# The last layer's input product as 15 block products in place of 18

## The chip, the cores and the metric

One core of one Trainium2 chip. The metric is the device time of one execution of the program in microseconds; lower is better. The kernel before took 1162.59 us (median of 3 runs, 1161.39 to 1164.65).

## The reference

Three layers in a row, on 4 x 768 tokens of width 384:

```python
attn_out = _attn_ref(q, k, v, beta)          # delta rule, 8 heads of 48
x = attn_out.transpose(0, 2, 1, 3).reshape(B * S, H * D)
# gated layer: d_ff 1536
xn = x / rms * rms_g
x = (silu(xn @ w_gate) * (xn @ w_val)) @ w_out
# last layer: d_ff 2048
h = x @ w_in
sp = np.where(h > 20.0, h, np.log1p(np.exp(np.minimum(h, 20.0))))
return (h * np.tanh(sp)) @ w_out2            # h * tanh(softplus(h)) is Mish
```

## The kernel before

A block is 64 positions of each of the 4 batches, T = 256 tokens; there are NR = 12. A matrix of 384 columns lies as KD = 3 tiles of 128 partitions. Every float32 operand of a large product is held as a high part (rounded to float32r) and a low part (the rest, by a subtraction on GpSimd), and a product of two operands takes three matmuls: high x high, high x low, low x high (`up`, lines 295 to 301).

`phase_b1` computes the attention row by row, with the first two of six pairs of gated column tiles (256 columns each) beside it, whose sums go to DRAM as `p_d`. `phase_b2` (line 1290) computes the other four pairs for each block: per pair 18 matmuls for the gate, Silu on ScalarE, 18 for the value, a multiplication (L357) and a cast (L360) on VectorE, the low part on GpSimd (L361), and then, after the first pair of the next block, the down product of the block before (72 matmuls). `finish` adds `p_d` (L1315), splits the sum (L1316, L1317) and stores both parts to DRAM (`yh_d`, `yl_d`). Beside it run the conversions of the last layer's weights, which come as 64-bit floats: `prepare_half` unpacks half a tile with one ScalarE instruction (L208) and four on VectorE (L212, L215, L220, L223), casts on ScalarE (L234) and subtracts on GpSimd (L237). All of w_in2 stays in SBUF; most of w_out2 goes through DRAM (`wq_d`) and is loaded during the last block.

`phase_c` is the last layer. A unit is a block and a pair of column tiles: 18 matmuls of 256 columns into one PSUM tile `ph` (a bank), Mish on ScalarE (L1362), a cast on VectorE (L1367), a subtraction on GpSimd (L1368), and 4 units later 12 matmuls of 384 columns (L1380 to L1382) that add to the block's two output banks. Three units are begun ahead of the last gated down product (`between`).

The order of the instructions on each engine is the order of the program text (`manual_schedule`); each engine executes its own in order, and so does each queue of DMA issues (SP's and ScalarE's). `merge` interleaves streams by the units that they yield: the gated products against the conversions, whose budget is CVB1.

## Time and profile before

| | |
|---|---|
| time of the profiled execution | 1162.49 us |
| its span, first to last instruction | 1160.8 us |
| median of the runs | 1162.59 us |
| attention, with gated pairs beside it | to about 441 us |
| gated layer, four pairs | about 441 to 741 us |
| last layer | about 741 us to the end |
| TensorE busy, matmuls | 1104.4 us, 14712 |
| VectorE, ScalarE, GpSimd busy | 616.4, 385.8, 414.5 us |

One execution, taken by the hardware profiler. Matmuls are pipelined: the duration shown is longer than the distance to the next. PE is TensorE's matmuls, PEld its weight loads, DVE VectorE, ACT ScalarE, POOL GpSimd, SP the engine that issues most DMAs. PEclk is the granted clock of TensorE as a share of full speed.

### The profile page before, as it was taken

Reading aid. Unit: us, or ns where it says so; the run is one execution under the profiler, and the core shown is the slowest. Engines: PE = TensorE matmul, PEld = TensorE weight load, DVE = VectorE, ACT = ScalarE, POOL = GpSimd, SP = SyncE. Lnnn points to the kernel's source line nnn. Section 1 sums busy time; section 2 is a strip of 40 time slices with the busy share of each in tenths; the row PEclk is TensorE's granted clock in tenths of the full one; section 3 lists DMA queues with packets and bytes.
Section 4 is the critical chain, followed back from the end, with each engine's and each line's share of the span. In section 5 each row is a group of like instructions: output and inputs, shape, how many; then the busy total and the mean of one; then the engine's idle time right before and its main releaser. Section 6 shows DMA issues by size and latency. Waiting matters only on the chain.

```text
span 1160.8 us, 33146 instructions
## 1 busy us (share of the span) xinstructions
PE 1104.4 (95%) x14712; PEld 1073.8 (93%) x14712; DVE 616.4 (53%) x1032; ACT 385.8 (33%) x829; POOL 414.5 (36%) x370
## 2 busy tenths in 40 slices
PE   5888689999999999999999999999999999999998
PEld 5777679989898899999999999999999999999998
DVE  7855998989898988767777622221111111111110
ACT  4465637576657742122222200111111111111110
POOL 2020234536342653444445422243333322233331
PEclk7666799999999999999999999999999999999999
DMA  9032323334136654344445423501111001111101
GB/s 167 5 79 63 111 56 85 85 84 97 45 91 175 202 180 137 120 145 132 165 150 188 153 82 128 209 19 41 42 42 41 28 22 34 42 41 42 41 3 26
DMA packets 130847, 104.48 MB, mean 90 GB/s; under 512 B 81008, under 2 KB 113264, under 8 KB 130704
## 3 DMA queue, kind: packets, MB, share of 16 engines
q1 hardware_dynamic: 118608, 78.77, 24.6%
q10 hardware_dynamic: 12096, 23.60, 6.0%
q8 instruction: 115, 1.88, 0.7%
q14 instruction: 28, 0.23, 0.1%
HBM read 69.31 MB, written 33.03 MB: 88 GB/s over the span
## 4 chain that ended last, share of the span: by engine, by line
PE 78%; DVE 12%; ACT 4%; issue 2%; POOL 1%; DMA 1%; SPq 1%; POOLq 0%; DVEq 0%; ACTq 0%
PE ph L300 6%; PE ph L299 6%; PE ph L301 6%; PE pd L1381 6%; PE pd L1382 6%; PE pd L1380 6%; PE pv L299 4%; PE pd L333 4%; PE pg L299 4%; PE pg L300 4%; PE pv L300 4%; PE pv L301 4%; PE pd L334 4%; PE pg L301 4%; PE pd L335 4%; DVE pr L700 2%
## 5 line engine op out<-in xcount | busy, mean ns | idle before, releaser
L1368 POOL TENSOR_TENSOR gl<-t,gh 128x512 fp32r<-128x512 f32 x96 | 123.7, 1290 | 266.1 <-DVE gh L1367 266.1
L1367 DVE CAST gh<-t 128x512 fp32r<-128x512 f32 x96 | 43.5, 456 | 328.8 <-ACT t L1362 328.8
L361 POOL TENSOR_TENSOR hl<-sg,hh 128x512 fp32r<-128x512 f32 x72 | 106.2, 1474 | 219.7 <-DVE hh L360 199.0
L1362 ACT ACTIVATE t<-ph 128x512 f32<-128x512 f32 x96 | 57.4, 598 | 346.5 <-PE ph L301 342.8
L300 PE MATMUL ph<-xl,wih 128*128 128x256 f32 x576 | 161.8, 281 | 0.0
L299 PE MATMUL ph<-xh,wih 128*128 128x256 f32 x576 | 161.7, 281 | 0.0
L301 PE MATMUL ph<-xh,wil 128*128 128x256 f32 x576 | 161.6, 281 | 0.0
L1381 PE MATMUL pd<-wql,gh 128*128 128x384 f32 x384 | 129.8, 338 | 0.0
L1382 PE MATMUL pd<-wqh,gl 128*128 128x384 f32 x384 | 129.7, 338 | 0.0
L1380 PE MATMUL pd<-wqh,gh 128*128 128x384 f32 x384 | 129.6, 337 | 0.0
L299 PE MATMUL pg<-xh,wgh 128*128 128x256 f32 x432 | 126.9, 294 | 0.4 <-ACT wgh L234 0.3
L299 PE MATMUL pv<-xh,wvh 128*128 128x256 f32 x432 | 126.0, 292 | 0.0
L301 PE MATMUL pg<-xh,wgl 128*128 128x256 f32 x432 | 123.2, 285 | 0.7 <-DVE wgl L237 0.6
L333 PE MATMUL pd<-hh,woh 128*128 128x256 f32 x420 | 120.8, 288 | 3.3 <-ACT par L1177 3.3
L300 PE MATMUL pg<-xl,wgh 128*128 128x256 f32 x432 | 123.2, 285 | 0.5 <-POOL xl L1127 0.5
L351 ACT ACTIVATE sg<-pg 128x512 f32<-128x512 f32 x72 | 43.2, 600 | 238.4 <-PE pg L301 225.2
L300 PE MATMUL pv<-xl,wvh 128*128 128x256 f32 x432 | 122.4, 283 | 0.0
L301 PE MATMUL pv<-xh,wvl 128*128 128x256 f32 x432 | 122.4, 283 | 0.0
L334 PE MATMUL pd<-hl,woh 128*128 128x256 f32 x420 | 118.9, 283 | 0.0
L335 PE MATMUL pd<-hh,wol 128*128 128x256 f32 x420 | 118.7, 282 | 0.0
L301 PEld LDWEIGHTS ph<-xh,wil 128*128 128x128 f32 x576 | 108.6, 189 | 0.0
L300 PEld LDWEIGHTS ph<-xl,wih 128*128 128x128 f32 x576 | 108.5, 188 | 0.0
(212 smaller groups left out, 2611.0 us busy)
## 6 DMA issues: line engine op xcount, KB each, us to landing
raw<-in_moe_w_out_dram SPq DMA_DIRECT2D x28, 384.0 KB, 3.6
raw<-in_moe_w_in_dram SPq DMA_DIRECT2D x16, 384.0 KB, 4.3
kh<-in_k_dram SPq DMA_DIRECT2D x24, 192.0 KB, 3.7
qp<-in_q_dram SPq DMA_DIRECT2D x24, 192.0 KB, 3.7
v<-in_v_dram SPq DMA_DIRECT2D x48, 96.0 KB, 3.3
raw<-in_moe_w_gate_dram SPq DMA_DIRECT2D x12, 384.0 KB, 4.6
raw<-in_moe_w_val_dram SPq DMA_DIRECT2D x12, 384.0 KB, 3.9
xh_d<-xh SPq DMA_DIRECT2D x12, 384.0 KB, 2.7
```

Of the source, the lines that this page charges most:

```text
L299: nc.tensor.matmul(ps[:, f, :], wh[:, kt, sl], xh[:, kt, :], start=(kt == 0), stop=False)
L300: nc.tensor.matmul(ps[:, f, :], wh[:, kt, sl], xl[:, kt, :], start=False, stop=False)
L301: nc.tensor.matmul(ps[:, f, :], wl[:, kt, sl], xh[:, kt, :], start=False, stop=(kt == KD - 1))
L333: nc.tensor.matmul(ps, wh[:, f, sl], hh[:, f, :], start=(i + f == 0), stop=False)
L334: nc.tensor.matmul(ps, wh[:, f, sl], hl[:, f, :], start=False, stop=False)
L335: nc.tensor.matmul(ps, wl[:, f, sl], hh[:, f, :], start=False, stop=last)
L361: nc.gpsimd.tensor_tensor(out=hl, in0=sg, in1=hh.bitcast(F32), op=ALU.subtract)
L1362: nc.scalar.activation(out=t, in_=ps, func=ACTF.Mish)
L1368: nc.gpsimd.tensor_tensor(out=gl, in0=t, in1=gh.bitcast(F32), op=ALU.subtract)
L1380: nc.tensor.matmul(ps, gh[:, f, sl], wh[:, f, :], start=(m + f == 0), stop=False)
L1381: nc.tensor.matmul(ps, gh[:, f, sl], wl[:, f, :], start=False, stop=False)
L1382: nc.tensor.matmul(ps, gl[:, f, sl], wh[:, f, :], start=False, stop=last and f == 1)
```

## The change

The blocks are taken in 6 pairs. For a pair and three column tiles of w_in2 (a triple, of which there are five), the input product is a product of 3x3 by 3x2 blocks: three column tiles by three k, and three k by two blocks. It was 18 block products and is computed by 15, each of a sum of weight blocks and a sum of input blocks, from which the six results come by 20 additions and subtractions. The sixteenth column tile is computed as before.

- The sums of weights are made in the gated layer (`prepare_forms`: 16 additions on VectorE for each triple, 18 blocks in all with the copies, split by ScalarE and GpSimd) and kept in DRAM, but for the first triple's. Those of triples 1 and 2 are loaded during the last gated block; those of 3 and 4 take turns in ten tiles and are loaded anew in every pair (`load_turn`).
- `finish` in the gated layer only adds. After every second block `forms_of` makes 10 sums of its 6 input blocks on VectorE, casts 16 blocks on ScalarE, subtracts on GpSimd and stores to `xf_d`; it runs beside the following gated blocks (`with_forms`), the last pair's beside the last layer. `load_group` brings them back three at a time.
- In the last layer a product is three matmuls into half a PSUM bank. The steps of `O_STEPS` (after which product, result, first operand, sign, second operand) follow on VectorE, with one copy on ScalarE. Mish works in place, the cast is ScalarE's, the output copy too. The output matmuls stand in a queue of tasks (one 128-token tile of one column tile: three matmuls) and are mixed in at 64 for 81 block products.
- All loads of the last layer are issued by SP. The first triple of the first pair stands where the three units stood.

```diff
+X_STEPS = (
+    (9, 0, ('x', 5), 1, ('x', 1)),
+    (12, 1, ('x', 1), 1, ('x', 0)),
...
+X_RAW = (6, 15, 8, 7, 14, 13)
+W_STEPS = (
+    (3, ('a', 1, 0), 1, ('a', 2, 1)),
+    (2, ('a', 1, 2), 1, ('a', 2, 1)),
+    (5, ('a', 0, 1), 1, ('a', 1, 0)),
...
+W_RAW = {1: (1, 2), 4: (2, 1)}
+O_STEPS = (
+    (1, ('u', 0), ('p', 1), 0, None),
+    (1, ('u', 1), ('u', 0), 1, ('p', 0)),
+    (2, ('u', 0), ('u', 0), 1, ('p', 2)),
+    (4, ('u', 0), ('u', 0), 1, ('p', 4)),
+    (4, ('u', 2), ('u', 0), -1, ('p', 3)),
+    (5, ('u', 3), ('u', 2), 1, ('p', 5)),
+    (6, ('u', 4), ('u', 3), 1, ('p', 6)),
+    (6, ('o', 2, 0), ('u', 4), -1, ('p', 4)),
+    (6, ('o', 1, 0), ('u', 1), -1, ('u', 3)),
+    (7, ('o', 1, 1), ('u', 2), -1, ('p', 7)),
+    (8, ('o', 1, 0), ('o', 1, 0), -1, ('p', 8)),
+    (9, ('u', 3), ('p', 9), 1, ('u', 4)),
+    (9, ('o', 2, 1), ('u', 0), 1, ('p', 9)),
+    (10, ('u', 2), ('p', 10), -1, ('u', 3)),
+    (11, ('u', 4), ('u', 2), -1, ('p', 11)),
+    (11, ('o', 0, 0), ('u', 1), 1, ('u', 4)),
+    (12, ('o', 0, 1), ('p', 12), -1, ('u', 2)),
+    (12, ('o', 2, 0), ('o', 2, 0), 1, ('u', 4)),
+    (13, ('o', 2, 1), ('o', 2, 1), -1, ('p', 13)),
+    (14, ('o', 2, 0), ('o', 2, 0), 1, ('p', 14)),
+)
+
+
 def plan(*streams):
 
...
+    xf_d = [dram.tile([128, 2, 16, T], F32, name=f"xf_d{i}") for i in range(NB)]
+    wi_d = {(s, g): dram.tile([128, 2, 3, 128], F32, name=f"wi_d{s}_{g}") for s in range(1, NS) for g in range(5)}
...
+    wq_d = [dram.tile([128, 2, 2, DM], F32, name=f"wq_d{m}") for m in range(NP2)]
...
+        def keep(g, forms):
+            slot = slot_of(g)
+            nc.scalar.copy(slot[:, 0], forms)
+            nc.gpsimd.tensor_tensor(out=slot[:, 1], in0=forms, in1=slot[:, 0].bitcast(F32), op=ALU.subtract)
+            if (s, g) in wi_d:
+                nc.sync.dma_start(out=wi_d[s, g], in_=slot.bitcast(F32))
...
+            elif i == 2:
+                F = [w2i.tile([128, 3, 128], F32, tag="F", name="F", bufs=6) for _ in range(6)]
+
+                def at(x):
+                    return blocks(x[1])[:, x[2]] if x[0] == "a" else F[x[1] // 3][:, x[1] % 3]
+
+                for j, (to, a, sign, b) in enumerate(W_STEPS):
+                    nc.vector.tensor_tensor(out=at(("w", to)), in0=at(a), in1=at(b), op=PLUS[sign])
+                    if j % 2:
+                        yield P["WS"]
+                for to, a in W_RAW.items():
+                    nc.scalar.copy(at(("w", to)), at(("a", *a)))
+                for g in range(5):
+                    keep(g, F[g])
+                    yield P["WK"]
+
+        return [one(i, 3 * s + i) for i in range(3 if s < NS else 1)]
...
-        op = st.enter_context(pool("op2", 1, side="right"))
...
+            if n % 2 == 0:
+                ys[n // 2] = [tpc.tile([128, 2, T], F32, tag="y", name="y", bufs=2 * KD) for _ in range(KD)]
...
+                nc.scalar.dma_start(out=ys[n // 2][o][:, n % 2], in_=p_d[n][:, o, :])
...
             def finish(o, ps):
-                y = pars.pop((n, o))
-                yh = op.tile([128, T], F32R, tag="yh", name="yh", bufs=2)
-                yl = op.tile([128, T], F32R, tag="yl", name="yl", bufs=1)
+                y = ys[n // 2][o][:, n % 2]
                 nc.vector.tensor_tensor(out=y, in0=y, in1=ps, op=ALU.add)
-                nc.vector.tensor_copy(yh, y)
-                nc.gpsimd.tensor_tensor(out=yl, in0=y, in1=yh.bitcast(F32), op=ALU.subtract)
-                nc.sync.dma_start(out=yh_d[n][:, o, :], in_=yh.bitcast(F32))
-                nc.sync.dma_start(out=yl_d[n][:, o, :], in_=yl.bitcast(F32))
+                if n % 2 and o == KD - 1:
+                    forming.append(forms_of(n // 2, ys.pop(n // 2)))
...
+        more = [prepare_forms(s, (lambda g: w0[g]) if s == 0 else staged) for s in range(NS + 1)]
+        more += [prepare_rows(m, staged) for m in range(NP2)]
+        cv = seq(cv, convs(more, early=True), early_loads())
...
+        todo = [lambda g=g: load_w(1, g, in_wb) for g in range(5)]
+        todo += [lambda m=m, x=x: load_q(m, x, in_wb) for m in (0, 1) for x in "hl"]
+        todo += [lambda g=g: load_w(2, g, in_wb) for g in range(5)]
+        todo += [lambda x=x: load_q(2, x, in_wb) for x in "hl"]
+
+        first = [lambda g=g: load_group(0, g) for g in range(4)] + [lambda: load_raw(0)]
...
         def used(n, m):
+            if m == FA:
+                next_x(n + 1)
+            if n >= 4 and (m - FA) % 2 and first:
+                first.pop(0)()
             if n == NR - 1:
-                for _ in range(min(2, len(free))):
-                    load_q(lambda *a, **kw: wbp[0].tile(*a, tag="wb", bufs=WE, **kw))
-
-        part_b = gated((ps_u, [ps_d], hp, tp), range(FA, NP1), range(NR), lambda n: xs[n], finish_b, next_x, between, used)
+                for _ in range(4):
+                    todo.pop(0)()
...
+        def with_forms(part):
+            for i, w in enumerate(part):
+                yield w
+                turn = i % 3 < 2 if len(ys) == 0 else i % 2
+                if forming and turn and next(forming[0], 0) is not None:
+                    forming.pop(0)
+
...
+    def forms_of(j, y):
+
+        us = {}
+
+        def keep(to, t):
+            fx = tpc.tile([128, 2, T], F32R, tag="fx", name="fx", bufs=4)
+            nc.scalar.copy(fx[:, 0], t)
+            nc.gpsimd.tensor_tensor(out=fx[:, 1], in0=t, in1=fx[:, 0].bitcast(F32), op=ALU.subtract)
+            nc.sync.dma_start(out=xf_d[j][:, :, to], in_=fx.bitcast(F32))
...
+        made = [(to, at(("x", i))) for i, to in enumerate(X_RAW)]
+        for _ in range(len(X_RAW) - 2):
+            keep(*made.pop(0))
+            yield
+        for to, u, a, sign, b in X_STEPS:
+            t = tpc.tile([128, T], F32, tag=f"xu{u}", name="xu", bufs=1)
+            nc.vector.tensor_tensor(out=t, in0=at(a), in1=at(b), op=PLUS[sign])
+            us[u] = t
+            made.append((to, t))
+            keep(*made.pop(0))
+            yield
+        while made:
+            keep(*made.pop(0))
+            yield
+
+    def load_group(j, g):
+        i = (5 * j + g) % 6
+        xg[j, g] = []
+        for x, tag in enumerate(("xh", "xl")):
+            if i < 4:
+                t = w2i.tile([128, 3, T], F32R, tag="gx", name="gx", bufs=8)
+            else:
+                t = xp.tile([128, 3, T], F32R, tag=tag, name="gx", bufs=XB)
+            nc.sync.dma_start(out=t.bitcast(F32), in_=xf_d[j][:, x, 3 * g:3 * g + 3])
+            xg[j, g].append(t)
...
     def phase_c():
         st = ExitStack()
-        units = [(n, m) for n in range(NR) for m in range(NP2)]
...
+        by_end = sorted(range(3), key=lambda i: max(n for n, o in enumerate(O_STEPS) if o[1][:2] == ("o", i)))
+        fs = [3 * s + i for s in range(NS - 1) for i in by_end] + [3 * NS] + [3 * NS - 3 + i for i in by_end]
...
+        pairs = [tpc.tile([128, 2, T], F32, tag="fx", name="ou", bufs=4) for _ in range(2)]
+        ou = [pairs[i // 2][:, i % 2] for i in range(4)] + [tpc.tile([128, T], F32, name="ou4")]
+
+        def half_bank():
+            i = halves[0]
+            halves[0] += 1
+            if i % 8 < 4:
+                banks[i % 4] = ps_u.tile([128, 2, T], F32, tag="u", name="ph")
+            return banks[i % 4][:, i % 8 // 4]
+
+        def finish(j, f, t):
+            nc.scalar.activation(out=t, in_=t, func=ACTF.Mish)
+            held.append((j, f, t))
+            if ready[0]:
+                split()
...
+        def split_one(j, f, t):
+            gh, gl = [hp.tile([128, 2, T], F32R, tag=x, name=x) for x in ("gh", "gl")]
+            nc.scalar.copy(gh, t)
             nc.gpsimd.tensor_tensor(out=gl, in0=t, in1=gh.bitcast(F32), op=ALU.subtract)
-
...
+        def down(j, f, tt, gs):
+            if f == fs[0] and tt == 0:
+                acc[:] = [ps_d.tile([128, DM], F32, tag="d", name="pd") for _ in range(4)]
+            gh, gl = (g[:, tt * 128:tt * 128 + 128] for g in gs)
+            wh, wl = (w[:, f % 2, :] for w in W["q", f // 2])
+            ps, last = acc[tt], f == fs[-1]
+            nc.tensor.matmul(ps, gh, wh, start=(f == fs[0]), stop=False)
+            nc.tensor.matmul(ps, gh, wl, start=False, stop=False)
+            nc.tensor.matmul(ps, gl, wh, start=False, stop=last)
+            if last:
+                ob = sums(NS * j + NS).rearrange("p a t -> p (a t)")[:, :DM]
+                nc.scalar.copy(ob, ps)
+                for b in range(2):
+                    t0 = (tt % 2 * 2 + b) * S + (2 * j + tt // 2) * C
+                    nc.sync.dma_start(out=out[t0:t0 + C, :], in_=ob[b * 64:(b + 1) * 64])
+
+        def beside(weight):
+            debt[0] += weight * 64.0 / 81.0
+            while debt[0] >= 1.0:
+                debt[0] -= 1.0
+                if not tasks:
+                    debt[0] = 0.0
+                    break
+                down(*tasks.pop(0))
+
...
+        def triple(j, s):
+            outs, place = {}, {}
+            steps = list(O_STEPS)
+
+            def at(x):
+                if x[0] == "p":
+                    return place[x[1]]
+                if x[0] == "u":
+                    return ou[x[1]]
+                if x[1] not in outs:
+                    outs[x[1]] = sums(NS * j + s)
+                return outs[x[1]][:, x[2]]
+
+            left = [sum(o[1][:2] == ("o", i) for o in O_STEPS) for i in range(3)]
+            for p in range(15):
+                g, k = divmod(p, 3)
+                xh, xl = (t[:, k] for t in xg[j, g])
+                wh, wl = (t[:, k] for t in wt[s][g])
+                ps = place[p] = half_bank()
+                nc.tensor.matmul(ps, wh, xh, start=True, stop=False)
+                nc.tensor.matmul(ps, wh, xl, start=False, stop=False)
+                nc.tensor.matmul(ps, wl, xh, start=False, stop=True)
+                whole = []
+                while steps and steps[0][0] <= p:
+                    _, to, a, sign, b = steps.pop(0)
+                    if b is None:
+                        nc.scalar.copy(at(to), at(a))
+                    else:
+                        nc.vector.tensor_tensor(out=at(to), in0=at(a), in1=at(b), op=PLUS[sign])
+                    if to[0] == "o":
+                        left[to[1]] -= 1
+                        if left[to[1]] == 0:
+                            whole.append(to[1])
+                yield p
+                if p == 1:
+                    while ended:
+                        finish(*ended.pop(0))
+                for i in whole:
+                    (ended if p == 14 else wholes).append((j, 3 * s + i, outs[i]))
+                while wholes:
+                    finish(*wholes.pop(0))
+
+        def single(j):
+            t = sums(NS * j + NS - 1)
+            w, = wt[NS]
+            ps = [half_bank() for _ in range(2)]
+            for i in range(2):
+                for k in range(KD):
+                    g, c = divmod(X_RAW[2 * k + i], 3)
+                    xh, xl = (v[:, c] for v in xg[j, g])
+                    wh, wl = (v[:, k] for v in w)
+                    nc.tensor.matmul(ps[i], wh, xh, start=(k == 0), stop=False)
+                    nc.tensor.matmul(ps[i], wh, xl, start=False, stop=False)
+                    nc.tensor.matmul(ps[i], wl, xh, start=False, stop=(k == KD - 1))
+                nc.scalar.copy(t[:, i], ps[i])
+                yield i
+            finish(j, 3 * NS, t)
+
+        for _ in triple(0, 0):
+            pass
         yield
...
+        wc = [lambda m=m, x=x: load_q(m, x, wbp[-1].tile) for m in (7, 6) for x in "hl"]
+        wc.append(lambda: load_w(NS, 0, wbp[-1].tile))
...
+        ready[0] = True
+        split()
+        for j in range(NB):
+            for s in range(NS):
+                if s == NS - 1:
+                    for _ in single(j):
+                        beside(3)
+                    if j + 1 < NB:
+                        load_raw(j + 1)
+                if s == 1 and j + 1 < NB:
+                    load_group(j + 1, 0)
+                for p in triple(j, s) if j + s else ():
+                    beside(1)
+                    if p % 5 == 0:
+                        next(late, None)
+                    if p % 3 == 2:
+                        if s == 0 and j:
+                            load_turn(NS - 2, p // 3)
+                        if s == NS - 2:
+                            load_turn(NS - 1, p // 3)
+                        if wc:
+                            wc.pop(0)()
+                        if s == NS - 1 and j + 1 < NB and p < 12:
+                            load_group(j + 1, p // 3 + 1)
+        while ended:
+            finish(*ended.pop(0))
+        while tasks:
+            down(*tasks.pop(0))
         st.close()
```

## Rows read from the trace of the kernel before

**Rows 1.** Windows: us, busy time of each engine with instructions, PEclk, DMA share, GB/s.

```profile
461.00:665.00 204.00, 204.00 (x1703) 204.00 (x1702) 144.75 (x232) 44.81 (x90) 94.96 (x86) 1.00 0.46 149
...
741.40:1156.60 415.20, 414.91 (x2955) 414.58 (x2953) 59.08 (x128) 58.55 (x97) 127.25 (x100) 1.00 0.12 37
...
740.00:745.00 5.00, 5.00 (x44) 5.00 (x44) 1.11 (x2) 2.10 (x3) 1.34 (x2) 1.00 0.89 342
```

**Rows 2.** Instruction groups, last layer (700 to 1161 us): busy us, mean ns | idle before.

```profile
L300 PE MATMUL ph<-xl,wih 128*128 128x256 f32 x576 | 161.8, 281 | 0.0
...
L1368 POOL TENSOR_TENSOR gl<-t,gh 128x512 fp32r<-128x512 f32 x96 | 123.7, 1290 | 266.1 <-DVE gh L1367 266.1
...
L1362 ACT ACTIVATE t<-ph 128x512 f32<-128x512 f32 x96 | 57.4, 598 | 346.5 <-PE ph L301 342.8 <-DMA xl<-yl_d 3.6
```

**Rows 3.** Timeline of TensorE in the last layer: start us, us, engine line.

```profile
1041.93 0.28 PE L299 MATMUL ph<-xh,wih 128*128 128x256 f32 x1
...
1044.07 0.33 PE L1380 MATMUL pd<-wqh,gh 128*128 128x384 f32 x1
...
1046.18 0.28 PE L299 MATMUL ph<-xh,wih 128*128 128x256 f32 x1
```

**Rows 4.** Groups, VectorE, gated layer (461 to 665 us).

```profile
L223 DVE SCALAR_TENSOR_TENSOR t<-raw,t 128x384 int32<-128x384 int32 x30 | 33.7, 1125 | 1.0
L215 DVE TENSOR_SCALAR t<-t 128x384 int32<-128x384 int32 x30 | 32.0, 1067 | 1.0
L357 DVE TENSOR_TENSOR sg<-sg,pv 128x512 f32<-128x512 f32 x32 | 21.9, 685 | 31.9 <-PE pv L301 30.4 <-ACT t L208 1.5
L220 DVE SCALAR_TENSOR_TENSOR t<-raw,t 128x384 int32<-128x384 int32 x30 | 20.5, 685 | 0.2
L360 DVE CAST hh<-sg 128x512 fp32r<-128x512 f32 x32 | 13.7, 428 | 1.1
L212 DVE TENSOR_SCALAR t<-t 128x384 f32<-128x384 f32 x30 | 10.6, 352 | 0.0
L1315 DVE TENSOR_TENSOR par<-par,pd 128x256 f32<-128x256 f32 x24 | 10.1, 420 | 23.0 <-PE pd L335 22.9
```

**Rows 5.** Single lines, VectorE and GpSimd: ns min/median/max, first and last start us.

```profile
L652 DVE TENSOR_TENSOR PT<-p,mpos x2: 662/666/671, 48.2 to 48.8; 128x512 f32<-128x512 f32 x2
...
L237 DVE TENSOR_TENSOR wgl<-t,wgh x6: 551/558/560, 115.7 to 370.0; 128x384 fp32r<-128x384 f32 x6
...
L215 DVE TENSOR_SCALAR t<-t x68: 359/780/1360, 102.7 to 656.9; 128x384 int32<-128x384 int32 x68
...
L223 DVE SCALAR_TENSOR_TENSOR t<-raw,t x68: 557/559/1542, 103.7 to 661.4; 128x384 int32<-128x384 int32 x68
...
L1317 POOL TENSOR_TENSOR yl<-par,yh x36: 726/735/989, 464.8 to 757.6; 128x256 fp32r<-128x256 f32 x36
```

**Rows 6.** Groups, whole span, ScalarE.

```profile
L1177 ACT COPY par<-pd 128x256 f32<-128x256 f32 x33 | 12.3, 373 | 37.9 <-PE pd L335 35.1 <-issue 2.5
...
L234 ACT CAST wih<-t 128x384 fp32r<-128x384 f32 x16 | 8.1, 506 | 1.2 <-DVE t L220 0.8 <-DVE t L223 0.4
...
L351 ACT ACT_TABLE_LOAD x1 | 1.3, 1283 | 0.0
L1362 ACT ACT_TABLE_LOAD x1 | 1.3, 1283 | 1.0 <-issue 1.0
```

**Rows 7.** Timeline in the gated layer, VectorE and GpSimd.

```profile
505.70 1.35 DVE L215 TENSOR_SCALAR t<-t 128x384 int32<-128x384 int32 x1
...
505.54 1.29 POOL L361 TENSOR_TENSOR hl<-sg,hh 128x512 fp32r<-128x512 f32 x1 [1.43 <-DVE hh L360]
```

**Rows 8.** Groups, GpSimd, gated layer (461 to 665 us).

```profile
L361 POOL TENSOR_TENSOR hl<-sg,hh 128x512 fp32r<-128x512 f32 x31 | 42.6, 1374 | 68.5 <-DVE hh L360 68.5
L1317 POOL TENSOR_TENSOR yl<-par,yh 128x256 fp32r<-128x256 f32 x24 | 19.4, 807 | 33.7 <-DVE yh L1316 14.7 <-DMA yl_d<-yl 11.6 <-issue 3.6
L237 POOL TENSOR_TENSOR wil<-t,wih 128x384 fp32r<-128x384 f32 x16 | 17.3, 1083 | 4.9 <-ACT wih L234 4.9
```

More of the change, by code (lines that the diff above doesn't have):

```diff
@@ L226, in prepare_half, with part @@
         yield
+    def prepare_half(half, get_pool, key, cut, act, low_by, kw):
+        src, nk, nf = cut
+        rows_split = nk == 2
+        def part(a):
+            return a[:, half:half + 1, :] if rows_split else a[:, :, half * 128:half * 128 + 128]
+        nk1 = 1 if rows_split else nk
+        ts = []
+        yield from value(part(src), nk1, act, ts)
         if half == 0:
```

200 lines of the change are left out of this document (121 added, 79 removed), and 13 rows, old and new, of the table W_STEPS.

## Prediction

> **What bounds the kernel now.** I read the page's slices first, to find where TensorE's line turns solid, then a table of windows over the two solid stages, then instruction groups, then timelines. In the windows [rows 1] see two stretches in which TensorE is busy all the time at a granted clock of 1.00: the gated layer (204.00 us of 204.00) and the last layer (414.91 of 415.20). The other engines differ: VectorE works 144.75 us of the first but only 59.08 of the second, GpSimd 94.96 and 127.25, ScalarE 44.81 and 58.55. No matmul group of the last layer has idle time before it, while ScalarE and GpSimd sit idle ahead of their work until TensorE or VectorE releases it [rows 2]. So in both stages each matmul more or less is its own length more or less, as long as the others keep up.
>
> The length is the distance between starts, not the 281 ns shown as busy, since matmuls overlap. In the timeline [rows 3], 18 matmuls of 256 columns start within 2.14 us (118.9 ns each), the next 12 of 384 within 2.11 (175.8 ns). Other such runs of 12 give 2.08, so I use 174.6. Check: 1728 x 0.1189 + 1152 x 0.1746 + 72 x 0.1189 (the last gated down product, which lies inside) = 205.5 + 201.1 + 8.6 = 415.2 us, the whole window.
>
> **The change part by part.** *Removed matmuls.* Per pair of blocks, the input product was 16 column tiles x 3 k x 2 blocks x 3 = 288 matmuls of 256 columns. Now five triples of 15 products x 3 make 225, the single sixteenth tile 18: together 243. 45 x 6 pairs = 270 fewer, so 270 x 0.1189 = 32.1 us. The 1152 matmuls of the output product stay, with the same operand sizes. All of that lies on the path that sets the end.
>
> *Sums behind the products.* A triple gives VectorE 19 additions (a twentieth step is ScalarE's copy). 16 read one PSUM operand of 128x256, as L1315 does now: 0.420 us [rows 4]. Three read SBUF twice. For these the trace has 0.558 at 384 columns and 0.666 at 512 [rows 5], a slope of 0.84 ns a column, so about 0.45 at 256. One triple: 16 x 0.42 + 3 x 0.45 = 8.1 us. TensorE's share of a triple is 45 x 0.1189 + 11.85 output tasks (15 x 64/81) x 3 x 0.1746 = 5.35 + 6.2 = 11.55 us, or 0.77 per product. VectorE would be 70% busy and keep up on average. ScalarE per pair: 16 Mish at 0.60 [rows 2], 16 casts of 512 columns at some 0.6 (0.506 at 384), 7 PSUM copies at 0.373 [rows 6], 4 output copies near 0.5: 24 us of 62. GpSimd keeps its 16 x 1.29 = 20.6.
>
> What can stall TensorE is PSUM. The eight halves lie in four banks. A product whose turn opens a new tile needs the readers of the products four and eight before it. Four products are about 3.1 us, and VectorE's backlog stays under 0.6, save at one place: product 4 is read again in the second addition of step 6, some 1.05 us after product 6 ends (two additions of 0.42 and hand-overs of about 0.1). Product 8 could start 1.23 us after that end if an output task follows both 6 and 7, but after 0.71 if one is skipped: 0.35 us lost, in some 4 of 10 triples, where product 8 opens a tile (half of them): 2 us in all. The Trainium skill's PSUM page (PSUM — Partial Sum Buffer, "PSUM bank collisions raise a hardware error") says to guard PSUM by bank, not by address, for two engines on one bank. The tiles ph, pg and pv of before are read only whole, so no row shows a half read while the other is written. By that rule product 8 waits in every triple, and the term is 4 us. Bounds without it: 0, and one lost half microsecond in each of 29 triples, 14. I take 3.
>
> *First triple.* It stands alone ahead of the last gated down product, with no output tasks to fill: 5.35 us of matmuls against VectorE's 8.1, behind the last gated multiply and cast (0.685 + 0.43 [rows 4]). Followed by hand, product 8 waits till 4.3 us (instead of 2.9), and the fifteenth ends 1.9 us late. Bounds 0.5 and 8.1 - 5.35 = 2.8. I take 1.9; the down product behind it (8.6 us) lets VectorE catch up.
>
> *Hand-over.* The casts for the first output tasks get their space only when the last down product has read it. Cast 0.6, GpSimd's subtraction 1.29, hand-overs: 2.1 us, of which two products and a first matmul cover 1.0. Cost 1.1, bounds 0 and 2.1. Later tasks have 4 or more others queued in front of each (the order gives 4 to 10 left at every step), about 3.9 us, against a chain of 0.42 + 0.6 + 0.6 + 1.29 and hand-overs, 3.2.
>
> *Gated layer.* TensorE's work is unchanged: 216 matmuls, 25.7 us a block. Beside it, VectorE loses the yh casts and gains 80 additions of weights (128x128, about 0.33 by the same slope) and 50 of the input (0.45); a last 10 fall into the next stage. Conversions now spread over all 12 blocks (their units add up to some 189 of the 192 that the merge allots): 32 x (0.352 + 0.359 + 0.557 + 0.559) = 58.5 us. Per block: 4 x (0.685 + 0.428) + 3 x 0.420 + 58.5/12 + 80 x 0.33/12 + 5 x 0.45 = 15.0 us. But these instructions wait for GpSimd. At 505.70 an L215, 0.359 us when free, takes 1.35 because GpSimd's subtraction began at 505.54 and lasted 1.29 [rows 7]. In the stretch, L223, L215 and L220 average 1.125, 1.067 and 0.685 against 0.559, 0.359 and 0.557 undisturbed [rows 4, 5]: 1.40 us for each of 30, or 5.3 a block (7.94 blocks), 45% of GpSimd's 12.0 us a block. GpSimd will have 4 x 1.29 + 8 x 0.735 + 42 x 1.08/12 = 14.8 us [rows 2, 5, 8]. At 45% VectorE loses 6.6 and needs 21.6 of 25.7: it keeps up, with bursts (16 weight additions at a time). The chain behind the last pair (multiply, cast, subtraction, 2.4 us) has about 6 us until TensorE needs it. I take 2 us; bounds 0 and, if all of GpSimd's time were lost, 29.8 - 25.7 = 4.1 us in 10 blocks, 41.
>
> The Trainium skill's SBUF page (SBUF — State Buffer, "Who interferes with whom") says VectorE and GpSimd share one port pair as an exclusive lock, taken by VectorE instructions with two SBUF inputs or in a 2-port mode, not by one with a PSUM operand. By that rule the 130 new additions from SBUF are all exposed and the 16 of a triple are free. The trace agrees: L357 and L1315, with one PSUM operand, stay at 0.685 and 0.420.
>
> *Transfers.* Each pair reloads 10 weight groups of 384 KB, 5 input groups of 768 KB, 256 KB raw, and stores the output: 8.7 MB in 62 us, 141 GB/s, 230 at the worst. The engines moved 342 in the window at 740 [rows 1], and a group has about 12 us until use: nothing, or 1 us a pair at worst. The loads leave ScalarE's queue for SP's, where stores waiting for GpSimd stand ahead of loads by no more than a few us.
>
> *Sum*, against the profiled execution's 1162.5 (span 1160.8; median of the runs 1162.59): 1162.5 - 32.1 = 1130.4; + 3 + 1.9 + 1.1 + 2 = 8. Result 1138.
>
> **The rivals.** *A: the additions set the pace.* In the last layer GpSimd lies on 3.2 x 1.29 = 4.1 us of a triple; if each of the three SBUF additions waits for a whole subtraction, VectorE needs 8.1 + 3.9 = 12.0 against 11.55, and 29 triples lose 0.45 each, 13 us, besides the 5 elsewhere: 1149. For it: the 1.35 above. Against: 3 hits of 3 where conversions show 45%.
>
> *B: slower.* In the gated layer each GpSimd subtraction stops a VectorE instruction for its whole length. VectorE then needs 29.8 us a block and becomes the bound: 1130.4 + 41 + 6 = 1177. It decides from 72% ((25.7 - 15.0)/14.8) upward of GpSimd's time lost; at 45% it costs nothing, and what is left of the gain is gone at 26 us, 2.6 a block. For it: VectorE is the second busiest there, and a pair gets 16 subtractions of 256 columns in place of 6. Against: the idle time that L357 and L1315 still wait for TensorE [rows 4].
>
> *C: the change does less than it says because ScalarE reloads tables.* Mish and copies alternate 96 times; if each turn loaded (1.28), ScalarE would need 24 + 41 = 65 us a pair against 62, at least 1157. Against: 16 casts for w_in2 stand between Silus that have a single load [rows 6].
>
> **How the numbers follow.** The forecast, 1131 to 1145, has 0.74; A (1145 to 1155) 0.13; B 0.09; C and anything else 0.04. The range of 8 in 10 is 1131 (waits close to none) to 1150, which takes in most of A. A measurement here tells 0.3%, 3.5 us, from no change. Faster: forecast, A, and a part of the rest: 0.86; same 0.04; slower 0.10.
>
> **What would show it.** 14442 matmuls in place of 14712; TensorE still without idle time at 118.9 and 174.6 ns, clock 1.00; the last layer some 26 us shorter, the gated layer's length unchanged within 3; VectorE from 14% to about 70% busy in the last layer; one table load for Mish. Gaps before product 8 of a triple would show the bank waits, gaps before gated matmuls B. I am wrong if TensorE waits over 20 us in all.

## The result

The changed kernel takes 1143.01 us (median of 5 runs, 1140.14 to 1144.35), the one before 1162.59 beside it (5 runs, 1160.94 to 1164.65): a ratio of 0.9827, 95% interval 0.9806 to 0.9847. Run again on another occasion it took 1145.53 (1140.02 to 1145.85), ratio 0.9834 [0.981, 0.9857]. The forecast was 1138, with 1131 to 1145 for its own case. The profiled execution took 1143.4 us, span 1141.7.

The page's busy times of the kernel after: TensorE has 14442 matmuls, 270 fewer than before, and VectorE works more.

```profile
PE 1081.7 (95%) x14442; PEld 1046.5 (92%) x14442; DVE 844.6 (74%) x1586; ACT 510.7 (45%) x1107; POOL 475.8 (42%) x440
```

Windows of the kernel after, with the columns of [rows 1]: the stretch of the gated layer that answers to 461 to 665, and the last layer from its first input product to its last matmul.

```profile
465.00:669.00 204.00, 204.00 (x1702) 203.99 (x1701) 164.55 (x281) 65.87 (x155) 126.39 (x123) 1.00 0.69 231
744.80:1134.80 390.00, 389.01 (x2684) 384.42 (x2682) 238.70 (x585) 148.38 (x274) 137.22 (x113) 1.00 0.46 146
```

TensorE is still solid in both. VectorE goes from 144.75 to 164.55 in the first and from 59.08 to 238.70 (61%) in the second.

Groups of the kernel after in the last layer, as [rows 2]; L1661 is the line of all 19 additions of a triple, and its groups differ by their operands (`ph` is in PSUM, `ou` and `t` in SBUF).

```profile
L1599 POOL TENSOR_TENSOR gl<-t,gh 128x512 fp32r<-128x512 f32 x96 | 123.9, 1292 | 246.9 <-ACT gh L1598 200.6 <-issue 24.7 <-DVE t L1661 10.6
L1661 DVE TENSOR_TENSOR ou<-ou,ph 128x256 f32<-128x256 f32 x210 | 88.4, 421 | 118.0 <-ACT ou L1659 68.2 <-PE ph L1654 39.4
L1587 ACT ACTIVATE t<-t 128x512 f32<-128x512 f32 x96 | 60.9, 634 | 185.2 <-DVE t L1661 180.1 <-DVE ou L1661 4.9
...
L1652 PE MATMUL ph<-gx,wr 128*128 128x256 f32 x180 | 51.0, 284 | 0.5 <-DVE t L1661 0.2
...
L1661 DVE TENSOR_TENSOR t<-ou,ou 128x256 f32<-128x256 f32 x30 | 23.6, 787 | 2.5
...
L1661 DVE TENSOR_TENSOR t<-t,ou 128x256 f32<-128x256 f32 x30 | 13.1, 437 | 0.0
L1661 DVE TENSOR_TENSOR t<-ou 128x256 f32<-128x256 f32 x30 | 12.5, 418 | 0.0
```

Additions with a PSUM operand take 421 ns. Of the three with SBUF operands alone, two take 437 and 418 in the mean; one takes 787, and 426 in the one triple where no subtraction of GpSimd runs as it starts. The small group of TensorE (L1652) waits for an addition: that is the new wait.

Three starts of matmuls cut the span of each trace into four stretches: the last matmul of `phase_b1` (it belongs to the gated down product that runs beside the attention), the first input product of the last layer, and the last matmul of all. What the forecast expected is the kernel before with the prediction's terms put in.

| stretch | before | expected | after |
|---|---|---|---|
| to the last product of the attention part | 439.08 | 439.08 | 440.42 |
| from there to the first input product of the last layer | 302.44 | 304.44 | 304.42 |
| from there to the last matmul | 414.45 | 388.35 | 389.92 |
| behind the last matmul | 4.81 | 4.81 | 6.92 |
| span | 1160.8 | 1136.7 | 1141.7 |

The first row has nothing to do with the change: over all executions profiled here that mark lies anywhere between 436.69 and 444.15 us, in kernels that don't differ ahead of it. In the two profiled executions of the changed kernel it differs by 3.7 us and the span by 3.4. So the experiments below are read by the other three rows, beside their time.

### The profile page after: what moved, and what is told of

The parts are those of the page before. It is cut to its first block, busy times and chain, and to the rows that moved or that the text cites. A ratio compares the mean times of both kernels' runs of the same rounds, so it can differ in the third digit from the quotient of the medians.

```text
span 1141.7 us, 34465 instructions
## 1 busy us (share of the span) xinstructions
PE 1081.7 (95%) x14442; PEld 1046.5 (92%) x14442; DVE 844.6 (74%) x1586; ACT 510.7 (45%) x1107; POOL 475.8 (42%) x440
## 4 chain that ended last, share of the span: by engine, by line
PE 71%; DVE 15%; issue 4%; ACT 4%; DMA 3%; POOL 2%; SPq 1%; POOLq 0%; DVEq 0%; ACTq 0%
PE pd L1610 6%; PE pd L1609 6%; PE pd L1611 6%; PE ph L1652 5%; PE ph L1653 5%; PE ph L1654 5%; PE pd L453 3%; PE pv L419 3%; PE pd L454 3%; PE pd L455 3%; PE pg L419 3%; PE pg L420 3%; PE pg L421 3%; PE pv L421 3%; PE pv L420 3%
## 5 line engine op out<-in xcount | busy, mean ns | idle before, releaser
L1661 DVE TENSOR_TENSOR ou<-ou,ph 128x256 f32<-128x256 f32 x210 | 88.4, 421 | 118.0 <-ACT ou L1659 68.2
L1587 ACT ACTIVATE t<-t 128x512 f32<-128x512 f32 x96 | 60.9, 634 | 185.2 <-DVE t L1661 180.1
L1609 PE MATMUL pd<-wqh,gh 128*128 128x384 f32 x288 | 97.4, 338 | 0.0
L1610 PE MATMUL pd<-wql,gh 128*128 128x384 f32 x288 | 97.3, 338 | 0.0
L1611 PE MATMUL pd<-wqh,gl 128*128 128x384 f32 x288 | 97.2, 337 | 0.0
L419 PEld LDWEIGHTS pg<-xh,wgh 128*128 128x128 f32 x432 | 83.5, 193 | 2.6 <-ACT wgh L303 0.7
L419 PEld LDWEIGHTS pv<-xh,wvh 128*128 128x128 f32 x432 | 82.8, 192 | 2.1
L420 PEld LDWEIGHTS pg<-xl,wgh 128*128 128x128 f32 x432 | 83.6, 194 | 1.0 <-POOL xl L1247 0.9
L453 PEld LDWEIGHTS pd<-hh,woh 128*128 128x128 f32 x420 | 79.7, 190 | 5.1 <-ACT par L1297 3.7
L421 PEld LDWEIGHTS pg<-xh,wgl 128*128 128x128 f32 x432 | 83.4, 193 | 1.0 <-DVE wgl L306 0.8
```

Source lines behind the costliest of these rows:

```text
L419: nc.tensor.matmul(ps[:, f, :], wh[:, kt, sl], xh[:, kt, :], start=(kt == 0), stop=False)
L420: nc.tensor.matmul(ps[:, f, :], wh[:, kt, sl], xl[:, kt, :], start=False, stop=False)
L421: nc.tensor.matmul(ps[:, f, :], wl[:, kt, sl], xh[:, kt, :], start=False, stop=(kt == KD - 1))
L453: nc.tensor.matmul(ps, wh[:, f, sl], hh[:, f, :], start=(i + f == 0), stop=False)
L1609: nc.tensor.matmul(ps, gh, wh, start=(f == fs[0]), stop=False)
L1610: nc.tensor.matmul(ps, gh, wl, start=False, stop=False)
```

## The experiments

Each was timed beside the kernel before, and its ratio is to that. Three numbers of each profiled execution are used: G, from the attention part's last product to the first input product; L, from there to the last matmul's start; E, what stands behind that. Before: 302.44, 414.45, 4.81; after: 304.42, 389.92, 6.92.

**Is the price of a matmul right, and does TensorE set the pace?** One kernel is the one before with 270 matmuls of the input product left out of the computation (three in each of its first 90 units of 96); the other is the changed one with the matmuls of three products of each triple issued twice, 270 more.

```diff
 # kernel before: `up` written out, three of the six matmuls high x low of a unit left out
-up(ps, W["i", m], f, *xs[n])
...
+if u >= 90 or (f, kt) not in ((0, 1), (1, 0), (1, 1)):
+    nc.tensor.matmul(ps[:, f, :], wh[:, kt, sl], xl[:, kt, :], start=False, stop=False)
...
 # changed kernel
+if p in (2, 10, 13):
+    nc.tensor.matmul(ps, wh, xh, start=True, stop=False)
+    nc.tensor.matmul(ps, wh, xl, start=False, stop=False)
+    nc.tensor.matmul(ps, wl, xh, start=False, stop=True)
```

> The kernel before with nothing of the change but the number of matmuls: 3 of the 18 matmuls of the input product of 90 of the 96 units are left out (one low x high part each, part of the computation), 270 in all. Theory (each matmul is worth its distance of 118.9 ns and nothing else bounds the last layer): 1162.5 - 32.1 = 1130.4, within 1 us. Rival (the ScalarE, VectorE or GpSimd chain behind a unit, or the loads, become the bound when a unit shrinks from 4.25 to 3.9 us): more than 1133.

> The three matmuls of products 2, 10 and 13 of every triple are issued twice (the second time from the start, so that the result stays): 9 x 30 = 270 more matmuls, as many as the kernel before had, with everything else of the change kept. Theory (TensorE sets the pace of the last layer, the rest of the change costs some 11 us of which 5 are waits of the first triple and before product 8): the time rises by 270 x 0.119 = 32 us, less some of the waits, to 1170 to 1176, slower than before by 8 to 13 us. Rival A of the prediction (VectorE's additions set the pace): a good part of the 32 us is hidden, time under 1165.

Fewer matmuls alone: 1130.55 us, 0.9722 [0.9689, 0.9755]; L is 381.98, 32.5 less (priced at 32.1). The changed kernel with as many matmuls as before: 1174.85, 1.0103 [1.0071, 1.0136]; L is 421.64, 31.7 more. So TensorE pays for each matmul in the changed last layer too, the additions don't set its pace (rival A falls), and all the rest of the change costs about 12 us of time, against 8 in the sum.

**The waits before product 8.** In the changed kernel the 29 triples behind the first lose 3.13 us at product 8 (nearly all in 13 of them, 0.1 to 0.43 us each) and nothing at any other product. Both edits let product 8 off product 4's last addition: one reads product 4 an addition earlier, the other gives each product a PSUM tile, and so a bank, of its own.

```diff
+(5, ('o', 2, 0), ('u', 3), -1, ('p', 4)),
...
-(6, ('o', 2, 0), ('u', 4), -1, ('p', 4)),
+(6, ('o', 2, 0), ('o', 2, 0), 1, ('p', 6)),
 # the other kernel
-if i % 8 < 4:
-    banks[i % 4] = ps_u.tile([128, 2, T], F32, tag="u", name="ph")
-return banks[i % 4][:, i % 8 // 4]
+return ps_u.tile([128, 2, T], F32, tag="u", name="ph")[:, 0]
```

> One addition is rearranged: the third result's first half is begun as u3 - p4 in step 5 and gets p6 in step 6, so that product 4 is read for the last time one step earlier; VectorE has 20 additions a triple instead of 19. Theory (the waits before product 8, 3.1 us in 29 triples of the changed kernel, come from the late second read of product 4 and nothing else): TensorE's lost time before product 8 falls under 0.5 us, nothing moves to another product, and the time falls by about 3 us to 1140. Rival (VectorE is simply behind at that point, whichever product it reads): the extra 0.42 us addition keeps the waits or moves them to products 9 to 11, at 3 us or more, and the time stays at 1143 or rises.

> Each product gets a PSUM tile of its own (a whole bank, four in turn) in place of half of a shared one: a product then always waits for the readers of the product four before it. Theory (waits go by bank: with half banks, too, every product waits for the readers of the fourth before it, whichever half it takes): nothing changes, 3.1 us lost before product 8 and 1143 within 1.5 us. Rival (halves are told apart, and half of the products wait only for the eighth before): waits before product 8 roughly double, some 3 us more, 1146.

Reading earlier: 1141.28, 0.9822 [0.9786, 0.9858]; the loss before product 8 is gone (under 0.05 us) and moved nowhere, L is 386.96. Whole banks: 1140.56, 0.9795 [0.9761, 0.983]; also gone, L is 386.59, where I had expected no change, since in half the triples product 8 opens a new tile that would be product 4's. It isn't: with whole banks product 8 starts while product 4 is still being read. VectorE and TensorE of the changed kernel in one triple (start us, us), then of the kernel with whole banks in the same triple. In the first kernel product 4 has the first half of a bank here and product 8 the second half of the same one.

```profile
805.92 0.42 DVE L1661 TENSOR_TENSOR ou<-ou,ph 128x256 f32<-128x256 f32 x1
806.37 0.42 DVE L1661 TENSOR_TENSOR t<-ou,ph 128x256 f32<-128x256 f32 x1
...
806.43 0.33 PE L1611 MATMUL pd<-wqh,gl 128*128 128x384 f32 x1
806.84 0.19 PEld L1652 LDWEIGHTS ph<-gx,wr 128*128 128x128 f32 x1 [0.40 <-DVE t L1661]
806.85 0.39 PE L1652 MATMUL ph<-gx,wr 128*128 128x256 f32 x1
```

```profile
805.14 0.42 DVE L1659 TENSOR_TENSOR t<-ou,ph 128x256 f32<-128x256 f32 x1
...
805.20 0.34 PE L1609 MATMUL pd<-wqh,gl 128*128 128x384 f32 x1
805.38 0.28 PE L1650 MATMUL ph<-gx,wr 128*128 128x256 f32 x1
```

In the first, L1611 starts at 806.43, the next matmul could at about 806.60, and product 8 (L1652) starts at 806.85, just behind the addition that ends at 806.79 and reads product 4; the profile names it as what product 8's weight load waited for. In the second it starts at 805.38, 0.18 behind the matmul ahead and inside the same addition (805.14 to 805.56).

**The end.** The last pair's copies go to VectorE, and half of the last stores leave from ScalarE's queue.

```diff
-nc.scalar.copy(ob, ps)
+(nc.vector.tensor_copy if j == NB - 1 else nc.scalar.copy)(ob, ps)
...
-nc.sync.dma_start(out=out[t0:t0 + C, :], in_=ob[b * 64:(b + 1) * 64])
+by = nc.scalar if j == NB - 1 and b else nc.sync
+by.dma_start(out=out[t0:t0 + C, :], in_=ob[b * 64:(b + 1) * 64])
```

> Only the last pair's output is treated otherwise: VectorE copies it instead of ScalarE, and the stores of every second half are issued by ScalarE instead of SP. Theory (the end is 2.1 us longer than before, 6.9 us after the last matmul's start against 4.8, because eight stores of about 0.6 us each are issued one after the other by SP): the stretch from the last matmul's start to the end falls to 4.5 to 5 us and the time by about 2 us to 1141. Rival (the landing of the last store, or the four copies, set the end): the stretch stays within 0.5 us of 6.9.

1142.6, 0.9823 [0.9795, 0.9852]. E is 4.93 against 6.92. The time alone would not show it: this profiled execution left the attention part at 444.15. SyncE's issues at the end (start us, us, how many) in the kernel before, after (with ScalarE's copies), and here:

```profile
1155.87 2.40 SPq L1388 DMA_DIRECT2D out_dram<-ob  x4
```

```profile
1133.55 2.12 ACT L1614 COPY t<-pd 128x384 f32<-128x384 f32 x4 [3.50 <-PE pd L1611]
1134.05 4.97 SPq L1617 DMA_DIRECT2D out_dram<-t  x8
```

```profile
1137.73 2.40 SPq L1618 DMA_DIRECT2D out_dram<-t  x4
```

About 0.6 us a store: the edit changes the copies too, but in the changed kernel these are done at 1135.67 and the issues of the stores go on without a gap to 1139.02. So it is the row of eight that holds the end; with four, E is within 0.2 us of the kernel before.

**The gated layer.** Its 2.0 us are waits at one place, the down product at 672 us (TensorE's waits, 441 to 1141 us: who waits, for whom, us, times, longest).

```profile
PE pd L454 <- POOL hl L481: 1.2, 1, 1.2
PE ph L1652 <- DVE ou L1661: 0.5, 2, 0.3
PE pd L453 <- DVE hh L480: 0.2, 1, 0.2
```

Three kernels ask what makes them: conversions spread otherwise over the blocks, GpSimd's subtraction of each split of the input issued twice, and GpSimd's subtractions of w_out2's rows left out.

```diff
 # other costs in the plan
-WK=2.0,
-CW=2.0,
+WK=1.2,
+CW=2.4,
 # twice
+for _ in range(2):
     nc.gpsimd.tensor_tensor(out=fx[:, 1], in0=t, in1=fx[:, 0].bitcast(F32), op=ALU.subtract)
 # left out
-nc.gpsimd.tensor_tensor(out=slot[:, 1], in0=ts[0], in1=slot[:, 0].bitcast(F32), op=ALU.subtract)
+nc.scalar.copy(slot[:, 1], ts[0])
```

> Only the pace in the gated layer: the units of the conversions go from 2.0 to 2.4 and those of the weight sums' low parts from 2.0 to 1.2, so that the conversions of w_out2, which now crowd at 640 to 680 us (VectorE busy 38.98 of 40), are spread wider. Theory (the 2.0 us at 672 us come from that crowd): VectorE's busiest 40 us fall to 36 or less and TensorE waits under 0.5 us in the gated layer, time 1141. Rival (the wait follows the input sums, which come in the same part of every second block): it stays at 2 us or moves to another block.

> GpSimd makes the low part of each input sum twice (the same subtraction again): 16 more subtractions of 128x256 a pair of blocks, 5.9 us of GpSimd a gated block. Theory (the 2.0 us that the gated layer lost at about 672 us come from VectorE and GpSimd excluding each other; GpSimd's time rises from 14.8 to 20.7 us of 25.7 a block, VectorE loses 9 or 10 in place of 6.6 and comes to 24 or 25): the slack is used up and the gated layer loses 10 to 30 us in TensorE's waits for hh and hl; time 1153 to 1173. Rival (the loss comes from stores and ScalarE's waits for their buffers, the exclusion has room left): the gated layer loses 2 to 5 us, time below 1148.

> The low part of the converted rows of the last layer's weights is left out of the computation: ScalarE copies the high part in its place, so GpSimd loses those subtractions from the gated layer and does all else. Theory: the wait of about 2.0 us ahead of one down product at 672 us comes from GpSimd, which delivers hl late there; without these subtractions the waits of the gated layer are under 0.5 us and the time is 1141 us. Rival: the wait is VectorE's (its queue is nearly full in that stretch) or the stores', and stays at 1.5 us or more, time 1143 us.

The other plan: 1145.4, 0.9837 [0.9808, 0.9865]; G is 307.42, and the loss rose to 4.98 us, at five blocks' ends. Windows 561 to 601 of after and of this one (columns as in [rows 1]):

```profile
561.00:601.00 40.00, 40.00 (x336) 39.99 (x335) 36.45 (x67) 12.16 (x30) 25.80 (x26) 1.00 0.87 302
```

```profile
561.00:601.00 40.00, 39.00 (x323) 38.59 (x323) 34.84 (x58) 11.36 (x27) 26.14 (x26) 1.00 0.85 289
```

TensorE stands 1.0 us here with VectorE at 34.84 of 40, and not at all with 36.45: how full VectorE is over 40 us does not decide by itself. But the plan did not do what it was for, the fullest of VectorE's windows still holds 38.15 (601 to 641), so what the crowd of conversions costs stays open.

Subtractions twice: 1171.39, 1.0062 [1.005, 1.0074], slower than before; G is 328.9 and L 392.96. Left out: 1140.83, 0.9804 [0.9778, 0.9829]; G is 302.50 and the waits 0.09. Windows 640 to 680 of after and of this one:

```profile
640.00:680.00 40.00, 38.60 (x320) 38.19 (x319) 38.98 (x57) 14.96 (x35) 28.77 (x26) 1.00 0.89 290
```

```profile
640.00:680.00 40.00, 40.00 (x336) 40.00 (x335) 35.24 (x61) 19.05 (x45) 19.19 (x18) 1.00 0.90 301
```

With 9.6 us less of GpSimd's work VectorE does more instructions (61 for 57) in less time (35.24 for 38.98). So GpSimd's load makes that wait; how much of it goes through VectorE these windows don't tell. The doubled kernel shows where it ends; windows of it, then its waits from 441 us to the last gated block:

```profile
481.00:521.00 40.00, 37.90 (x316) 37.69 (x315) 26.42 (x49) 11.65 (x28) 24.88 (x28) 1.00 0.49 164
...
641.00:681.00 40.00, 37.24 (x296) 36.83 (x295) 39.17 (x57) 14.50 (x33) 30.36 (x30) 0.96 0.79 258
681.00:721.00 40.00, 33.64 (x265) 33.23 (x264) 39.35 (x49) 12.47 (x29) 37.10 (x38) 0.91 0.70 224
```

```profile
PE pd L454 <- POOL hl L481: 12.3, 5, 4.6
PE pd L453 <- DVE hh L480: 2.8, 2, 1.8
PE pv L419 <- DVE sg L477: 2.1, 1, 2.1
```

These are eight waits, 17.2 us in all. Behind four of them the granted clock falls to 0.50 for a while: 76 matmuls that wait for nothing start some 0.21 us after the one ahead in place of 0.12, and that is another 7.7 us of the 26.5 by which G is longer than before.

VectorE is full in the last two windows, and TensorE also waits in the first, where VectorE has 13 us to spare. The timeline of GpSimd and VectorE there tells why (start us, us):

```profile
514.09 1.20 POOL L321 TENSOR_TENSOR ws<-F,ws 128x384 fp32r<-128x384 f32 x1
515.25 1.67 POOL L1492 TENSOR_TENSOR fx<-y,fx 128x256 fp32r<-128x256 f32 x2
516.88 1.01 POOL L321 TENSOR_TENSOR ws<-F,ws 128x384 fp32r<-128x384 f32 x1
517.85 3.08 POOL L1492 TENSOR_TENSOR fx<-xu,fx 128x256 fp32r<-128x256 f32 x4
520.89 1.57 POOL L481 TENSOR_TENSOR hl<-sg,hh 128x512 fp32r<-128x512 f32 x1
...
513.13 1.28 DVE L480 CAST hh<-sg 128x512 fp32r<-128x512 f32 x1
...
519.42 0.93 DVE L1504 TENSOR_TENSOR xu<-y,xu 128x256 f32<-128x256 f32 x1 [3.10 <-POOL fx L1492]
```

VectorE had made `hh` by 514.41; the low part starts at 520.89, behind eight GpSimd instructions queued ahead of it, and VectorE itself stands 3.10 us. TensorE's matmul on `hl` came 3.78 us late, at 522.52. Three of the eight waits, 10.5 us, stand behind such a row on GpSimd.

**The first triple.** Its products are interleaved with the last gated down product instead of standing ahead of it.

```diff
-between()
-yield from (down_by_pair if len(pairs) == FA else down)(*prev)
...
+for _ in range(3):
+    between()
+for w in down(*prev):
+    yield w
+    for _ in range(2):
+        between()
```

> The first triple no longer stands alone: three of its products come ahead of the last gated down product, the other twelve between its matmuls, two after every twelve. Theory (the first triple loses 2.05 us because VectorE needs 8.1 us beside 5.35 of matmuls): with 13.9 us of matmuls in all VectorE keeps up; from the first product to the last gated down matmul 13.9 to 14.2 us in place of 16.0, time 1141. Rival (the wait moves: the last pair's hl is needed earlier, or the first output tasks come before their casts): the gain is under 1 us.

1139.68, 0.9788 [0.9746, 0.9829]; L is 388.38: 1.5 of the first triple's 2.05 come back, with one wait of 0.3 us for GpSimd's first subtraction in their place.

**What else slows the last layer.** After the waits, 2.4 us are left: without the starts that a wait delays, matmuls of 256 columns start 0.1196 us apart in the mean where they were 0.1183, those of 384 0.1756 for 0.1751. Here the combining of the products is left out of the computation: six steps of a triple stay, each a ScalarE copy of one product, so VectorE has next to nothing in the last layer.

```diff
+O_STEPS = ((7, ('o', 1, 1), ('p', 7), 0, None), (8, ('o', 1, 0), ('p', 8), 0, None),
+    (11, ('o', 0, 0), ('p', 11), 0, None), (12, ('o', 0, 1), ('p', 12), 0, None),
+    (13, ('o', 2, 1), ('p', 13), 0, None), (14, ('o', 2, 0), ('p', 14), 0, None))
```

> The combining of the products in the last layer is left out of the computation: of the 20 steps of a triple six stay, each a ScalarE copy of one product into a half of an output tile (after products 7, 8, 11, 12, 13 and 14, the last ones that each half reads today), so VectorE has no addition in the triples and all matmuls are as before. What it is to tell: after the waits are taken out, each matmul of the last layer is still about 1 ns longer than in the kernel before (256 columns .1193 to .1206 us against .1183, 384 columns .1757 against .1748), some 2.4 us in all. Theory: VectorE's additions, on PSUM and SBUF beside the matmuls, slow TensorE a little; without them first input product to last matmul is 389.9 - 2.05 (first triple) - 3.1 (waits ahead of product 8) - 2.4 = 382.3 us, time about 1135 us, and the pace is back at .1183 and .1748. Rival: the pace has another cause (the loads, the alternation of short and long matmuls), stays at .119 to .1206 and .1757, and the stretch is 384.5 to 385 us, time about 1138 us.

1139.47, 0.9798 [0.9769, 0.9826]; L is 384.68 with no wait at all: the rival's number, not 382.3. Its window in the last layer:

```profile
760.00:1120.00 360.00, 360.00 (x2500) 360.00 (x2499) 7.13 (x11) 187.61 (x401) 131.36 (x109) 1.00 0.46 145
```

So VectorE's additions cost the first triple's 2.05 and the 3.13, together nearly the whole of 389.92 - 384.68 = 5.24, and the 2.3 left above 414.45 - 32.1 = 382.35 are none of theirs: the matmuls start 0.1194 and 0.1755 apart here. Neither of the two causes that the rival names fits this trace. The layer changes between short and long matmuls some 353 times each way in place of 91; but the first triple, which stands alone and changes not once, takes 5.41 us for its 45 matmuls, 0.1201 each, while the first triples of the later pairs change 22 times each and run at 0.1180 to 0.1183. Nor do the loads fit: a triple with 312 GB/s beside it (from 810.88) runs at 0.1181, one with 11 GB/s (from 833.72) at 0.1200. From the second on, each triple has the same pace in the kernel with all three edits below, to within 0.2 ns. So the slower pace is the program's and not chance; what in the program makes it stays open.

**All together, and the control.** Whole banks, the end's copies and stores, and the interleaved first triple in one kernel, beside the changed kernel once more.

> Three changes together: each of the 15 products in a PSUM bank of its own, the last pair's copies on VectorE with half of the last stores from ScalarE's queue, and the first triple interleaved with the last gated down product. By the single runs the first takes 3.3 us from the last layer, the second 2.0 from the end and the third 1.5 from the entry: 1143 - 6.8 = about 1136 us, below both kernels. In the trace: first input product to the last matmul about 385.5 us, 4.9 to 5.0 behind it. The rival, that the gains stand in each other's place (the first triple has waits of its own once its products are interleaved with the down product's): 1139 to 1141, with new waits ahead of products in the first triples.

> The changed kernel once more, to see what of a microsecond or two is its own. My theory: about 1143 us (1141 to 1146); the last product of the attention part ends anywhere between 436 and 444 us and carries the whole time with it, while the stretch from there to the first input product stays at 304.4 to 304.7 us, the waits in the gated layer at about 2.0 us, those of the last layer at about 5, and what stands behind the last matmul at 6.9. The rival, that the waits are chance: 0 in one execution and 4 in another.

Together: 1135.38 (1131.38 to 1140.39), 0.9761 [0.9734, 0.9788], below both kernels; L is 385.19, E 4.91, and of the last layer's waits the one for GpSimd's first subtraction is left (0.3 us, with 0.1 on the product behind it). G is 306.98: its gated layer lost 4.6 us at the same place (of which below). The gains in L and E add up. The control: 1145.53, G 304.92 with 2.5 us of waits at the same down product, L 389.68, E 6.95, and all 13 triples that wait before product 8 do so again, for the same times to within 0.02 us. So the waits before product 8 are the program's, not chance; the loss in the gated layer is at a fixed place, but its size is not: 2.0, 2.5 and, with all three edits, 4.6 us, in kernels that don't differ ahead of it.

## Why the prediction was right, and where it was off

**The removed matmuls** were priced right: 32.1 against 32.5 and 31.7 in two kernels.

**The additions** were: 19 sum to 8.29 us a triple in the groups above (and those not shown), 8.1 expected; VectorE is 61% busy over the last layer (about 70% said). Rival A had all three SBUF additions behind a whole subtraction; only one is delayed, and by the rest of a subtraction (787 ns for 426), and the first of the experiments shows that TensorE pays for its matmuls all the same.

**The waits before product 8** are 3.13 for 3, all at product 8, behind product 4's second addition, as the step said. The place was wrong: its 2 us came from triples where product 8 opens a tile, but 11 of the 13 triples that wait are those where product 8 takes the second half of a tile that product 4 has the first half of. An opened tile need not be the one that product 4 had: with whole banks product 8 starts while product 4 is still being read. So the 3, taken between 2 and the 4 of the rule by bank, is right in the cause and lucky in the size. The wait goes by bank, not by address: product 8 waits for a reader of the half of its bank that it does not write. Here the Trainium skill's PSUM page (PSUM — Partial Sum Buffer, "PSUM bank collisions raise a hardware error"), which says to guard PSUM by bank, agrees with the trace: with a bank of its own product 8 has no wait (0.0 us in 29 triples). A tile is a bank in these kernels, so no run tells a guard by tile from one by bank.

**The first triple** cost 7.40 against 5.35 us, 2.05 for 1.9.

**The hand-over** was 1.1 and is nothing. The step thought that the casts get their space when the last down product has read it, to its end. Timeline of the kernel after there:

```profile
759.70 1.36 ACT L1598 CAST gh<-t 128x512 fp32r<-128x512 f32 x2 [6.00 <-PE pd L455]
...
760.45 2.53 POOL L1599 TENSOR_TENSOR gl<-t,gh 128x512 fp32r<-128x512 f32 x2 [12.77 <-ACT gh L1598]
...
760.76 0.29 PE L455 MATMUL pd<-hh,wol 128*128 128x256 f32 x1
760.88 0.28 PE L1652 MATMUL ph<-gx,wi 128*128 128x256 f32 x1
...
761.48 0.29 PE L1654 MATMUL ph<-gx,wi 128*128 128x256 f32 x1
761.60 0.33 PE L1609 MATMUL pd<-wqh,gh 128*128 128x384 f32 x1
```

The first cast begins at 759.70, while that down product still has 1.2 us of matmuls to go; the first output task (L1609) follows two products without a gap.

**The gated layer** cost 2.0 for 2, where bursts meet; the 2 was picked between bounds of 0 and 41 and is matched by luck, as the 2.5 and 4.6 of the other executions show. VectorE works 20.7 us of a block's 25.7 (164.55 x 25.7 / 204; 21.6 expected), GpSimd 15.9 (14.8). Rival B's mechanism is real, and its point was set too high: it was to decide from 72% of GpSimd's time lost, over a mean block. The doubled kernel, whose GpSimd works 20.2 us a block (188.41 of 240), loses 24 us more than the changed one: 10.5 us of its waits stand behind the queue on GpSimd itself, and the slower clock behind the waits takes 7.7, neither of which the prediction had. Groups of the kernel after, 465 to 669 us, for two additions of 256 columns:

```profile
L1503 DVE TENSOR_TENSOR xu<-y,xu 128x256 f32<-128x256 f32 x10 | 9.6, 960 | 0.3 <-POOL fx L1491 0.3
...
L1430 DVE TENSOR_TENSOR y<-y,pd 128x256 f32<-128x256 f32 x24 | 9.9, 414 | 11.3 <-PE pd L455 11.3
```

Of the same size, the one with a PSUM operand takes 414 ns, the one from SBUF alone 960 in the mean and 410 at the least (x15, 441 to 745 us). The Trainium skill's SBUF page (SBUF — State Buffer, "Who interferes with whom") says that a VectorE instruction with two SBUF inputs contends with a GpSimd instruction that reads SBUF, and one with at most one SBUF input does not; the trace agrees.

**Not in the sum at all** were the end and the slower pace of the matmuls. The sum left the pace of the matmuls that stay as it was; they take 2.4 us more, and what causes it is not shown. The end: the output tiles now hold two batches in 128 rows, so the last pair makes eight stores where the last block made four, and SyncE issues them one after another: 2.1 us. With the pace's 2.4, the hand-over's -1.1, the first stretch's 1.3 and 0.3 of rounding in three terms, the span's 5.0 over the forecast is accounted for; that it is no more is in part because the hand-over was put too high.

**Rival C** falls: one table load stands before the 96 Mish of L1587. Loads don't hold TensorE: no wait of a matmul names a DMA.

## What to carry to other kernels

When multiplications are bought off with additions on an engine that has room, price the matmuls by the distance of their starts, and then look for the few places where a product is read late: give each product a bank, or order the reads, before counting averages. Read the slack of the helping engines in the fullest stretch, not over the stage: here VectorE had a fifth of its time left in the mean of the gated layer and 1.0 us of 40 where TensorE waited, and less load on GpSimd was enough to free it. And count the instructions of the very last step, each store too; there nothing hides them.

## What the hardware showed beside this

A wait can cost more than itself. In the kernel with all three edits TensorE waited 1.67 and 1.46 us at 674 and 676 us; then the mean granted clock of the window behind them was 0.63, with matmuls 0.21 us apart for 2.6 us at 0.50, the lower of its two levels (1.2 and 2.4 GHz):

```profile
672.00:676.00 4.00, 1.34 (x9) 0.93 (x8) 3.90 (x7) 0.37 (x1) 2.23 (x2) 0.94 0.99 309
676.00:680.00 4.00, 3.96 (x22) 3.96 (x23) 3.90 (x8) 1.59 (x4) 2.87 (x3) 0.63 0.94 289
680.00:684.00 4.00, 4.00 (x35) 4.00 (x34) 3.97 (x6) 1.58 (x4) 3.93 (x5) 1.00 0.98 362
```

Twelve matmuls at 0.21 for 0.12 us are 1.1 us more. In the control, waits of 0.86 and 1.46 at the same place left the clock at 1.00. In the doubled kernel such stretches came again and again, 7.7 us in all, which is the 0.91 and 0.96 in its windows above.
